# A transformer layer with conditioned norms: c first on its queue, the last tile in two column steps, one load for two chunks, and a new order of all engines

## The chip, the cores and the metric

The kernel runs on one core of a Trainium2 chip. The metric is the device time of one execution in microseconds (us). Where this text names engines: PE multiplies matrices (PEld is its loading of weights, which overlaps it), ACT is ScalarE, DVE is VectorE, POOL is GpSimd, SP is SyncE, which here only issues DMAs.

## What is computed

One layer over 2048 tokens of 448 features, in bf16: a local, dilated attention (16 heads of 28, 8 keys at a distance of 2 each) and a feed-forward of 1792, each behind a layernorm whose shift, scale and gate come from a small vector c.

```python
x = A_x                                             # (1, 2048, 448)
mod = (_silu(c) @ w_mod).reshape(c.shape[0], 6, 1, -1)
sa, ca, ga, sb, cb, gb = (mod[:, i] for i in range(6))
h = _layernorm(x) * (1 + ca) + sa
x = x + ga * _A_ref(h, A_wqkv, A_wo)                # q, k, v = h @ wqkv; softmax over keys s, s-2, ..., s-14; @ wo
h = _layernorm(x) * (1 + cb) + sb
x = x + gb * (_silu(h @ B_w1) @ B_w2)
```

## The kernel before

**Tiles.** The tokens are cut into 4 chunks of 512, each of 4 tiles of 128 rows (two neighbouring tokens share a partition, so even and odd tokens, which never attend to each other, are separate tiles). Everything stays in SBUF: x (`x_all`, 16 tiles), all weights, the queries and keys of all tokens (`qk`).

**Stages.** For each chunk `norm1` (L640) makes statistics on DVE (L497) or ACT (L501, L507), the root on POOL (L513), a normed copy `xn` (L523 to L527), its transpose on PE (chunk 0, L564) or by DMA (chunks 1 to 3, L588), and scale and shift (L571, L573, L593, L595). `project` (L659) multiplies h with the query and key weights (L668) and the value weights (L688). The query and key weights are first copied from `wqk` into `wp`, where each head of 28 columns is padded to 32 (`pad`, L601 to L606); the last 64 rows of both have a load of their own, `wqk3` (L381). Attention goes by 9 blocks of 112 queries and the two parities: `logits` (PE L716, exponentials on ACT L724, a mask on DVE L748), `values` (PE L774, a normalisation on DVE L779 and L780, a DMA transpose L784), `out_proj` (PE L804, DVE L807). The feed-forward goes by chunks: `ffn1` (PE L831, Silu on ACT L839), `ffn2` (PE L854, an add on DVE L859, a store L862). `last_tile` (L875) replaces `ffn2` for the last 128 rows: its output columns are in two accumulators of 224, one added to x on DVE (L892), the other with x already in it (a matmul with the identity, L882) copied on ACT (L895); one store follows (L898). The gates of the modulation are multiplied into `wo` (L916) and `w2` (L920); `mrow` (L477) is the row of modulations from which they come.

**Halves of rows.** 448 is three and a half times 128. The projections, `out_proj` and `ffn1` therefore use matmuls on 64 rows in pairs that run side by side: `phases` (L609) makes a "straight" part of 8 matmuls and a "crossed" part of 6, which waits (L630) until the straight part has left PE.

**Order.** Every step is an operation of `Plan` (L106) with a number. A search made offline wrote the order of all operations into `ORDER` (L44): the numbers in turn, with the engine where there is a choice (`v` is DVE, `a` is ACT) and the PSUM banks after slashes. `emit` (L205) issues them so. Each engine, and SP's queue of DMAs, runs its own operations in that order and waits by semaphore for what they need. The durations and the `lag` in the calls of `P.op` are for the search; where the order is written out they are not used. A second path (`safe`), which runs only if a softmax sum leaves its range, plans its order anew.

**First loads.** ACT's queue issues the second pair of tiles of x, then c (L368, L369), and loads the table for Silu (L370). SP's queue issues the first pair, the first half of `w_mod`, then weights and chunks of x, all by `load` (L361, L362). A DMA to chunk k of x is one of `ld_x` (L383).

Of the kernel before, what the change touches and what calls it, by code (L numbers as in the profile page):

```python
# [10 lines left out]
ALU = mybir.AluOpType  # L11
ACTF = mybir.ActivationFunctionType
# [21 lines left out]
NC = 4  # L34
# [203 lines left out]
def layer(ctx, tc, io, safe):  # L238
# [24 lines left out]
    def onet():  # L263
        return psum[:, P.bank("one"), :]
# [103 lines left out]
    act_q = [P.op(("none", 0.0), lambda o: nc.scalar.dma_start(**first_x(1)))]  # L368
    act_q.append(P.op(("none", 0.0), lambda o: nc.scalar.dma_start(out=c4[:], in_=c.rearrange("o (k p) -> (o k) p", p=KM)), act_q[-1:]))  # L369
    ld_c = [P.op(("none", 5200.0), lambda o: S.preload_act_table(ACTF.Silu), act_q[-1:])]  # L370
    ld_x = [[load(224, **first_x(0)), P.op(("none", 4400.0), none, act_q[:1])]]
# [11 lines left out]
    ld_x += [[load(448, x_all[:, 4 * k:4 * k + 4, :].rearrange("p (i t) d -> p i (t d)", t=2), x_view[k], late)] * 2 for k in range(1, NC)]  # L383
# [225 lines left out]
    def phases(mm, n, deps, split=False):  # L609
# [25 lines left out]
        return box, a, P.op(("pe", 3 * step), crossed, [a], mode=1, lag=300.0)  # L635
# [239 lines left out]
    def last_tile(k, j, u):  # L875

        box, n = {}, D // 2

        def part(o, f0, f1):
            if f0 == 0:  # L880
                box["ps"] = [onet(), onet()]
                T.matmul(box["ps"][1][:, 0:n], lhsT=ident[:], rhs=x_all[:, u, n:D], start=True, stop=False)  # L882
            for f in range(f0, f1):
                for i in range(2):
                    T.matmul(box["ps"][i][:, 0:n], lhsT=hid[:, k % 2, f % 2, f // 2, 128 * j:128 * j + 128], rhs=w2[:, f // 2 + 7 * (f % 2), n * i:n * i + n],  # L885
                             start=(f + i == 0), stop=(f == NF - 1))
# [4 lines left out]
        def add(o):  # L891
            V.tensor_tensor(out=box["o"][:, 0:n], in0=box["ps"][0][:, 0:n], in1=x_all[:, u, 0:n], op=ALU.add)  # L892

        def move(o):
            S.copy(out=box["o"][:, n:D], in_=box["ps"][1][:, 0:n])  # L895

        def store(o):
            nc.sync.dma_start(out=out_view[u // 4, u // 2 % 2, u % 2], in_=box["o"][:])  # L898
        prev = None
        for f0, f1 in ((0, 4), (4, 8), (8, 12), (12, 14)):  # L900
            need = silus[k][f0 // 2:f1 // 2] + w2_gated + ([x1_done[u]] if f0 == 0 else [])
            prev = P.op(("pe", 194.0 * (f1 - f0) + (98.0 if f0 == 0 else 0.0)), lambda o, f0=f0, f1=f1: part(o, f0, f1), need + [prev], take=("one", "one") if f0 == 0 else ())
            if f0 == 0:
                first = prev
# [119 lines left out]
```

## Time and profile before

| | us |
|---|---|
| median of three runs | 171.99 (170.29 to 173.71) |
| the profiled execution | 170.89 |
| its span, from first to last instruction | 169.2 |
| busy: PE, ACT, DVE, POOL | 160.8, 116.4, 99.1, 15.5 |

The profile is of one execution, so sums are made against its 170.89, of which 169.2 is the span. Times in its rows count from the start of the span. PE's matmuls are pipelined and their ends are modelled, so that PE can be marked busy while it is behind its pace; its pace is read from groups that run without a wait. In a row of a timeline stand start, length, engine, line, operation, tile written and tiles read, shape, count, and in brackets how long the engine was idle before it and what ended that.

The costliest groups of instructions are PE's in the feed-forward:

```profile
L831 PE MATMUL psum<-h,w 64*128 64x512 bf16 x392 | 43.7, 376 | 0.0
L854 PE MATMUL psum<-w,both 128*128 128x448 bf16 x210 | 42.1, 353 | 0.0
L839 ACT ACTIVATE both<-psum 128x1024 bf16<-128x1024 f32 x28 | 27.3, 1021 | 13.6 <-PE psum L831 13.6
```

Behind the bar stand busy time and the mean of one in ns (pipelined matmuls overlap, so the mean is longer than the distance from one to the next), then the idle time of the engine ahead of the group.

### The profile page before, as it was taken

How to read it: one execution, taken by the hardware profiler on the slowest of the kernel's cores; microseconds unless marked ns; L12 is line 12 of the kernel's file. 1: busy time of each engine (PE TensorE's matmuls, PEld its weight loads, DVE VectorE, ACT ScalarE, POOL GpSimd, SP SyncE). 2: the span in 40 equal slices, each digit the busy share in tenths (PEclk: the TensorE clock that was granted, in tenths of full speed). 3: DMA queues.
4: the chain of work that ended last, by engine and by line, in shares of the span. 5: the costliest groups of instructions: out<-in, count | busy, mean ns of one | idle time of the engine just before them, and what ended most of it. 6: DMA issues, size and time to landing. Idle time of an engine off the chain costs nothing.

```text
span 169.2 us, 4278 instructions
## 1 busy us (share of the span) xinstructions
PE 160.8 (95%) x1763; PEld 79.9 (47%) x1764; DVE 99.1 (59%) x259; ACT 116.4 (69%) x166; POOL 15.5 (9%) x38
## 2 busy tenths in 40 slices
PE   7878999999999999999999999999999999999990
PEld 2344444353465554554464454564444454444670
DVE  2788899999988859475476309972950405100120
ACT  3676999899779967879996989484429903248000
POOL 4313112010000410011000000021001100000000
PEclk9999999999999999999999999999999999999999
DMA  5994999859994453500614001226410061100022
GB/s 180 251 324 171 190 303 164 265 154 101 142 248 109 112 103 76 169 0 9 119 27 111 2 0 31 54 63 117 113 54 6 0 124 38 49 0 0 27 62 68
DMA packets 32312, 17.48 MB, mean 103 GB/s; under 512 B 24157, under 2 KB 31453, under 8 KB 32285
## 3 DMA queue, kind: packets, MB, share of 16 engines
q1 hardware_dynamic: 32132, 16.90, 42.9%
q8 instruction: 16, 0.26, 0.7%
q10 hardware_dynamic: 152, 0.23, 0.4%
q14 instruction: 12, 0.09, 0.2%
HBM read 9.12 MB, written 1.84 MB: 65 GB/s over the span
## 4 chain that ended last, share of the span: by engine, by line
PE 74%; DMA 9%; DVE 7%; ACT 5%; issue 2%; SPq 0%
PE psum L831 25%; PE psum L854 24%; PE psum L804 7%; PE psum L668 6%; DMA wqk<-in_A_wqkv_dram 5%; PE psum L688 4%; PE psum L774 4%; PE psum L716 2%; DMA x_all<-in_A_x_dram 2%; DMA oT<-o 2%; DVE p L748 2%; PE psum L885 2%; ACT both L501 1%; ACT wp L603 1%; DVE wqk L595 1%
## 5 line engine op out<-in xcount | busy, mean ns | idle before, releaser
L831 PE MATMUL psum<-h,w 64*128 64x512 bf16 x392 | 43.7, 376 | 0.0
L854 PE MATMUL psum<-w,both 128*128 128x448 bf16 x210 | 42.1, 353 | 0.0
L839 ACT ACTIVATE both<-psum 128x1024 bf16<-128x1024 f32 x28 | 27.3, 1021 | 13.6 <-PE psum L831 13.6
L724 ACT ACTIVATE p<-psum 128x896 bf16<-128x896 f32 (+1 forms) x36 | 31.7, 935 | 5.0 <-PE psum L716 4.7
L831 PEld LDWEIGHTS <-w 64*128 64x128 bf16 x392 | 19.3, 94 | 22.2 <-issue 0.7
L854 PEld LDWEIGHTS <-both 128*128 128x128 bf16 x210 | 19.6, 98 | 19.1 <-issue 1.6
L513 POOL TENSOR_TENSOR rs<-rs,negh 128x2 f32<-128x2 f32 x16 | 12.5, 778 | 118.0 <-DVE rs L510 82.6
L748 DVE TENSOR_TENSOR p<-p,maskb 128x1792 bf16<-128x1792 bf16 (+1 forms) x18 | 19.5, 1099 | 4.8 <-ACT p L724 4.8
L859 DVE TENSOR_TENSOR ot<-psum,x_all 128x448 bf16<-128x448 f32 x15 | 9.2, 618 | 20.2 <-PE psum L854 15.9
L668 PE MATMUL psum<-h,wp 64*128 64x512 bf16 x168 | 19.8, 377 | 0.5 <-ACT wp L603 0.4
L668 PEld LDWEIGHTS <-wp 64*128 64x128 bf16 x224 | 10.4, 94 | 12.8 <-ACT wp L603 0.9
L507 ACT ACTIVATE mrow<-x_all,mv 128x448 bf16<-128x448 bf16 x16 | 10.7, 668 | 3.4 <-DVE mv L504 3.0
L804 PE MATMUL psum<-wo,oT 64*128 64x448 bf16 x112 | 12.7, 350 | 0.1
L593 ACT ACTIVATE h<-h,modc 128x512 bf16<-128x512 bf16 x7 | 5.5, 806 | 10.2 <-DMA h<-xn 10.2
L672 ACT CAST qk<-psum 128x1024 bf16<-128x1024 f32 x12 | 12.0, 1018 | 0.6 <-PE psum L668 0.6
L688 PE MATMUL psum<-wv,h 64*128 64x448 bf16 x98 | 11.3, 350 | 1.2 <-DMA wv<-in_A_wqkv_dram 1.1
L807 DVE SCALAR_TENSOR_TENSOR x_all<-psum,x_all 128x448 bf16<-128x448 f32 x16 | 9.5, 619 | 3.6 <-PE psum L804 3.6
L780 DVE TENSOR_TENSOR o<-psum,rc 112x448 bf16<-112x448 f32 (+1 forms) x18 | 11.2, 624 | 0.6
L779 DVE RECIPROCAL rc<-psum 112x16 f32<-112x16 f32 (+1 forms) x18 | 4.5, 251 | 10.2 <-PE psum L774 9.5
L774 PEld LDWEIGHTS <-p 128*128 128x128 bf16 x288 | 8.2, 96 | 3.3 <-issue 1.7
L774 PE MATMUL psum<-v,p 128*128 128x29 bf16 x288 | 9.0, 176 | 0.0
L595 DVE TENSOR_SCALAR h<-h,modc 128x512 bf16<-128x512 bf16 x17 | 6.1, 406 | 4.8 <-DMA h<-xn 4.6
(95 smaller groups left out, 144.6 us busy)
## 6 DMA issues: line engine op xcount, KB each, us to landing
out_dram<-ot SPq DMA_DIRECT2D x16, 112.0 KB, 1.8
both<-in_w_mod_dram SPq DMA_DIRECT2D x1, 1568.0 KB, 8.4
x_all<-in_A_x_dram SPq DMA_DIRECT2D x3, 448.0 KB, 8.1
w<-in_B_w_dram SPq DMA_DIRECT2D x3, 448.0 KB
w<-in_B_w_dram SPq DMA_DIRECT2D x1, 896.0 KB, 7.0
both<-in_w_mod_dram SPq DMA_DIRECT2D x2, 392.0 KB, 5.7
w<-in_B_w_dram SPq DMA_DIRECT2D x1, 672.0 KB, 5.4
wv<-in_A_wqkv_dram SPq DMA_DIRECT2D x2, 224.0 KB, 8.5
```

The costliest lines, as they stand in the source:

```text
L513: G.tensor_tensor(out=rs[:, j:j + n], in0=rs[:, j:j + n], in1=negh[:, 0:n], op=ALU.pow)
L668: return T.matmul(ps[:, j, :], lhsT=w.rearrange("p h d -> p (h d)"), rhs=h[rows, :, t, 128:128 + CP], start=start, stop=stop)
L672: copy_on(o)(out=qk[:, :, g, :, s0:s0 + CP], in_=ps.rearrange("p j (t s) -> p j t s", t=2))
L688: T.matmul(ps[:, par, 0:D], lhsT=h[rows, par, t, b0:b0 + 128], rhs=wv[rows, t, :], start=start, stop=stop)
L724: S.activation(out=out_, in_=ps[:, :, 0:4 * nq].rearrange("p j (g q) -> p j g q", q=nq), func=ACTF.Exp, scale=SCALE)
L748: V.tensor_tensor(out=p, in0=p, in1=maskb[:, 1 if b == 0 else 0, 0:nq].unsqueeze(1).to_broadcast([128, H, nq]), op=ALU.mult)
L774: T.matmul(ps[:, h, 0:DH + 1], lhsT=p[:, at:at + 128], rhs=v[:, h, 0:DH + 1], start=True, stop=True)
L780: V.tensor_tensor(out=box["o"][0:nq, off:off + D].rearrange("p (h d) -> p h d", d=DH), in0=ps[0:nq, :, 0:DH], in1=r.unsqueeze(2).to_broadc ...
L804: T.matmul(ps[par][:, 0:D], lhsT=oT[rows, t, par, s0:s0 + 128], rhs=wo[rows, par, t, :], start=start, stop=stop)
L831: return T.matmul(ps[:, j, :], lhsT=w, rhs=h[rows, :, t, :], start=start, stop=stop)
L839: silus[k].append(P.op(("act", 904.0), lambda o, i=i, box=box: S.activation(out=hid[:, k % 2, :, i, :], in_=box["ps"], func=ACTF.Silu), [m ...
L854: T.matmul(box["ps"][:, 0:D], lhsT=hid[:, k % 2, f % 2, f // 2, 128 * j:128 * j + 128], rhs=w2[:, f // 2 + 7 * (f % 2), :], start=(f == 0) ...
```

## The change

1. On ACT's queue c is issued before the tiles of x. In the new order the Silu of c is ACT's first instruction.
2. Chunks 2 and 3 of x come in one DMA of 896 KB, where each had its own of 448.
3. `last_tile` has three accumulators, of 224, 112 and 112 columns. PE runs the first over all 14 steps, then the other two. The first is added on DVE and stored while PE works on the rest; of the rest one part is added on DVE and the other (with x in it by the identity matmul) copied on ACT, and a second store follows.
4. `ORDER` is another one throughout. On SP's queue `wqk3` comes behind the other `wqk` loads (before: ahead of `wv`). ACT, DVE, POOL and PE have other orders, and some operations with a choice are on the other engine: the cast of `mrow` is on DVE, the pad of `wqk3` on ACT.
5. `lag` and some durations for the search are other numbers.

```diff
 ORDER = (
-    "1 60/0 46 47 6 0 4 7 5 80 81 8 2 9 61 63 66 88 3 69 89 70/2 62 10 22 16 48 90 67 18 19 82 55 20 87 91 71 73/2 83 84 21 11 85v 74 97/3/4 86v 98 64 92 "
...
+    "1 0 4 58/0 5 78 7 2 8 44 45 79 46 59 6 9 10 22 3 67 68/2 23 69 61 20 86 18 19 71/2 87 88 49 50 80 21 64 60 65 85 89 11 72 12 81 63 82 83v 95/3/4 84v "
...
-    act_q = [P.op(("none", 0.0), lambda o: nc.scalar.dma_start(**first_x(1)))]
-    act_q.append(P.op(("none", 0.0), lambda o: nc.scalar.dma_start(out=c4[:], in_=c.rearrange("o (k p) -> (o k) p", p=KM)), act_q[-1:]))
+    act_q = [P.op(("none", 0.0), lambda o: nc.scalar.dma_start(out=c4[:], in_=c.rearrange("o (k p) -> (o k) p", p=KM)))]
+    act_q.append(P.op(("none", 0.0), lambda o: nc.scalar.dma_start(**first_x(1)), act_q[-1:]))
...
-    ld_x += [[load(448, x_all[:, 4 * k:4 * k + 4, :].rearrange("p (i t) d -> p i (t d)", t=2), x_view[k], late)] * 2 for k in range(1, NC)]
+    ld_x.append([load(448, x_all[:, 4:8, :].rearrange("p (i t) d -> p i (t d)", t=2), x_view[1], late)] * 2)
+    ld_x += [[load(896, x_all[:, 8:16, :].rearrange("p (k i t) d -> p k i (t d)", i=2, t=2), x_view[2:4].rearrange("c p i n -> p c i n"), late)] * 2] * 2
...
-        return box, a, P.op(("pe", 3 * step), crossed, [a], mode=1, lag=300.0)
+        return box, a, P.op(("pe", 3 * step), crossed, [a], mode=1, lag=230.0)
...
     def last_tile(k, j, u):
-        box, n = {}, D // 2
+        box, cut = {}, (0, D // 2, 3 * D // 4, D)
...
+            for f in range(f0, f1):
+                for i in range(i0, i1):
+                    T.matmul(box["ps"][i][:, 0:cut[i + 1] - cut[i]], lhsT=hid[:, k % 2, f % 2, f // 2, 128 * j:128 * j + 128], rhs=w2[:, f // 2 + 7 * (f % 2), cut[i]:cut[i + 1]],
+                             start=(f == 0 and i < 2), stop=(f == NF - 1))
...
+        for i0, i1 in ((0, 1), (1, 3)):
+            for f0, f1 in ((0, 8), (8, 14)):
...
+            if i0 == 0:
+                ot = P.op(("none", 0.0), hold, [first], take=("out",))
+                done = [P.op(("dve", 310.0), lambda o: add(o, 0), [prev, ot], give=((first, "one"),))]
+                sp(550.0, lambda o: store(o, 0, 1), done, dma=(390.0, 500.0, 250.0))
+            else:
+                ad = [P.op(("dve", 195.0), lambda o: add(o, 1), [prev, ot], give=((first, "one"),)), P.op(("act", 150.0), move, [prev, ot], give=((first, "one"),))]
+                sp(550.0, lambda o: store(o, 1, 3), ad, 1200.0, ((ot, "out"),), (390.0, 500.0, 250.0))
```

More of the change, by code (lines that the diff above doesn't have):

```diff
@@ L367, in first_x @@
         return dict(out=x_all[:, 2 * i:2 * i + 2, :].rearrange("p t d -> p (t d)"), in_=x_view[0, :, i, :])
[L368 to L371, printed above, removed]
+    act_q = [P.op(("none", 0.0), lambda o: nc.scalar.dma_start(out=c4[:], in_=c.rearrange("o (k p) -> (o k) p", p=KM)))]
+    act_q.append(P.op(("none", 0.0), lambda o: nc.scalar.dma_start(**first_x(1)), act_q[-1:]))
+    ld_c = [P.op(("none", 3900.0), lambda o: S.preload_act_table(ACTF.Silu), act_q[-1:])]
+    ld_x = [[load(224, **first_x(0)), P.op(("none", 4800.0), none, act_q[-1:])]]
     def load_mod(k0, k1, c0, c1, after=()):
@@ L875, in last_tile, with part @@
     def last_tile(k, j, u):
-        box, n = {}, D // 2
-        def part(o, f0, f1):
+        box, cut = {}, (0, D // 2, 3 * D // 4, D)
+        def part(o, f0, f1, i0, i1):
             if f0 == 0:
-                box["ps"] = [onet(), onet()]
-                T.matmul(box["ps"][1][:, 0:n], lhsT=ident[:], rhs=x_all[:, u, n:D], start=True, stop=False)
+                box.setdefault("ps", []).extend(onet() for _ in range(i0, i1))
+                if i1 == 3:
+                    T.matmul(box["ps"][2][:, 0:cut[3] - cut[2]], lhsT=ident[:], rhs=x_all[:, u, cut[2]:cut[3]], start=True, stop=False)
@@ L883, in part @@
             for f in range(f0, f1):
-                for i in range(2):
-                    T.matmul(box["ps"][i][:, 0:n], lhsT=hid[:, k % 2, f % 2, f // 2, 128 * j:128 * j + 128], rhs=w2[:, f // 2 + 7 * (f % 2), n * i:n * i + n],
-                             start=(f + i == 0), stop=(f == NF - 1))
+                for i in range(i0, i1):
+                    T.matmul(box["ps"][i][:, 0:cut[i + 1] - cut[i]], lhsT=hid[:, k % 2, f % 2, f // 2, 128 * j:128 * j + 128], rhs=w2[:, f // 2 + 7 * (f % 2), cut[i]:cut[i + 1]],
+                             start=(f == 0 and i < 2), stop=(f == NF - 1))
@@ L888, in hold, with add @@
         def hold(o):
             box["o"] = outb[o["slot"]["out"]]
-        def add(o):
-            V.tensor_tensor(out=box["o"][:, 0:n], in0=box["ps"][0][:, 0:n], in1=x_all[:, u, 0:n], op=ALU.add)
+        def add(o, i):
+            V.tensor_tensor(out=box["o"][:, cut[i]:cut[i + 1]], in0=box["ps"][i][:, 0:cut[i + 1] - cut[i]], in1=x_all[:, u, cut[i]:cut[i + 1]], op=ALU.add)
         def move(o):
-            S.copy(out=box["o"][:, n:D], in_=box["ps"][1][:, 0:n])
-        def store(o):
-            nc.sync.dma_start(out=out_view[u // 4, u // 2 % 2, u % 2], in_=box["o"][:])
@@ L899, in last_tile @@
[L899 to L904, printed above, removed]
-        ot = P.op(("none", 0.0), hold, [first], take=("out",))
-        ad = P.op(("dve", 310.0), add, [prev, ot], give=((first, "one"),))
@@ L907, in last_tile, with store @@
-        mv = P.op(("act", 242.0), move, [prev, ot], give=((first, "one"),))
-        sp(550.0, store, [ad, mv], 1200.0, ((ot, "out"),), (390.0, 500.0, 360.0))
+            S.copy(out=box["o"][:, cut[2]:cut[3]], in_=box["ps"][2][:, 0:cut[3] - cut[2]])
+        def store(o, i, n):
+            nc.sync.dma_start(out=out_view[u // 4, u // 2 % 2, u % 2][:, cut[i]:cut[n]], in_=box["o"][:, cut[i]:cut[n]])
+        prev, done = None, []
+        for i0, i1 in ((0, 1), (1, 3)):
+            for f0, f1 in ((0, 8), (8, 14)):
+                need = silus[k][f0 // 2:f1 // 2] + w2_gated + ([x1_done[u]] if f0 == 0 else [])
+                prev = P.op(("pe", 97.0 * (f1 - f0) + (50.0 if i0 and not f0 else 0.0)), lambda o, a=(f0, f1, i0, i1): part(o, *a), need + [prev], take=("one",) * (i1 - i0) if f0 == 0 else ())
+                if f0 == 0:
+                    first = prev
+            if i0 == 0:
[5 more added lines that the diff above has]
+                sp(550.0, lambda o: store(o, 1, 3), ad, 1200.0, ((ot, "out"),), (390.0, 500.0, 250.0))
```

44 rows, old and new, of the table ORDER are left out of this document.

## The prediction

> **What bounds the kernel now.** I read the totals first, then the chain of work that ended last, then the stretches.
>
> ```profile
> span 169.2 us, 4278 instructions
> PE 160.8 (95%) x1763; PEld 79.9 (47%) x1764; DVE 99.1 (59%) x259; ACT 116.4 (69%) x166; POOL 15.5 (9%) x38
> PE 74%; DMA 9%; DVE 7%; ACT 5%; issue 2%; SPq 0%
> ...
> 39.34 3.02 DMA oT<-o
> 42.41 0.93 PE psum L804 x7
> ...
> 165.11 0.37 DVE ot L892
> ...
> 42.40:165.10 122.70, 122.69 (x1315) 62.73 (x1315) 62.72 (x157) 80.76 (x108) 6.76 (x8) 1.00 0.31 68
> ```
>
> The first two rows are the page's totals, the third its chain of waits by engine; then three pieces of that chain in order of time (start, length, what). The last row is one stretch of the table by windows: of the 122.70 us between 42.40 and 165.10, PE is busy for 122.69, at a granted clock of 1.00, while DVE and ACT are busy for 62.72 and 80.76. The chain of waits says the same: from 42.41 on every piece is PE's, up to the last add. In these 123 us an edit gains only by giving PE less to do, and loses whatever it makes PE wait. The remaining 46 us are the head (PE waits for loads, then works with small stalls) and a tail of 4 us. The head, in the timeline of each engine, with two pieces of the chain from later on as the measure of PE's pace:
>
> ```profile
> 12.16 3.27 PE L688 MATMUL psum<-wv,h 64*128 64x448 bf16 x28 [1.05 <-DMA wv<-in_A_wqkv_dram]
> 15.86 7.97 PE L668 MATMUL psum<-h,wp 64*128 64x512 bf16 x70 [0.43 <-ACT wp L603]
> 23.76 0.73 PE L716 MATMUL psum<-qk 28*128 28x128 bf16 x16
> 28.31 0.40 PE L716 MATMUL psum<-qk 28*128 28x128 bf16 x16
> 37.42 1.04 PE L668 MATMUL psum<-wqk,wp 64*128 64x512 bf16 x8 [0.22 <-ACT qk L672]
> 41.94 1.39 PE L804 MATMUL psum<-wo,oT 64*128 64x448 bf16 x8
> ...
> 14.03 1.78 ACT L603 COPY wp<-wqk 128x896 bf16<-128x896 bf16 x2 [1.29 <-DMA wqk<-in_A_wqkv_dram]
> ...
> 14.73 0.39 DVE L603 COPY wp<-wqk 128x896 bf16<-128x896 bf16 x1 [0.79 <-DMA wqk<-in_A_wqkv_dram]
> ...
> 65.32 0.57 PE psum L804 x6
> 143.59 10.68 PE psum L831 x98
> ```
>
> PE starts the value projections at 12.16, when `wv` has landed, and the query and key projections at 15.86, when ACT has made its second padded copy of `wqk` (14.03 + 1.78 = 15.81). These copies waited for `wqk`: one part was there at 14.03, the other at 14.73. So the DMA of the weights sets 15.86.
>
> From there to 42.41 PE is marked busy but is not at its pace. At 10.68/98 = 0.109 us a matmul 70 projections need 7.63, and took 7.97 (0.34 lost); the logits at 23.76 took 0.73 where the like group at 28.31 took 0.40 (0.33); 0.22 is idle at 37.42; the output projection took 1.39 for 8 matmuls, where 8 need 0.57 × 8/6 = 0.76 (0.6 lost). That is 1.5 us which another order could win in this stretch, and no more.
>
> **The change, part by part.**
>
> *c first on ScalarE's queue, one table load less.* Two things happen to ACT: the tile of x on its queue is issued after c, and the Silu table is loaded before anything else, so that the first of two loads goes.
>
> ```profile
> 0.81 0.41 ACTq L368 DMA_DIRECT2D x_all<-in_A_x_dram  x1
> 1.25 0.58 ACTq L369 DMA_DIRECT2D c<-in_c_dram  x1
> 1.86 1.28 ACT L501 ACT_TABLE_LOAD   x1 [1.86 <-issue]
> 5.14 1.28 ACT L370 ACT_TABLE_LOAD   x1
> 9.46 2.84 ACT L571 ACTIVATE h<-psum,modc 128x256 bf16<-128x256 bf16 x6 [2.03 <-PE psum L564]
> ```
>
> The tile of x is issued about 0.6 later (c's issue took 0.58), and the second table load no longer stands between c and its silu (1.28). Both matter only for h at 9.46 to 12.30, and h is needed together with `wv` (12.16) and the padded `wqk` (15.86), so the net gain of 1.28 − 0.58 = 0.7 is hidden by the weights; I take 0. Were that cover gone, it would be worth up to 0.7; if h came later instead, 15.86 − 12.30 = 3.5 of cover are there, less the 3.3 of value projections that want h first.
>
> ```profile
> 14.00:15.00 1.00, 1.00 (x14) 0.61 (x11) 0.27 (x1) 0.97 (x2) 0.65 (x1) 1.00 0.39 142
> 15.00:16.00 1.00, 0.57 (x7) 0.11 (x4) 1.00 (x5) 1.00 (x2) 0.00 (x0) 1.00 0.19 67
> 16.00:17.00 1.00, 1.00 (x12) 0.44 (x10) 1.00 (x3) 1.00 (x3) 0.00 (x0) 1.00 0.05 18
> ...
> 30.57 0.56 ACT L477 CAST mrow<-psum 128x448 bf16<-128x448 f32 x1
> 16.41 0.62 DVE L497 BATCH_NORM_STATS2 st<-x_all 128x6 f32<-128x448 bf16 x1
> 16.51 0.58 ACT L501 ACTIVATE both<-x_all 128x448 bf16<-128x448 bf16 x1
> ```
>
> *The order of SP's queue: the small `wqk3` load moves from ahead of `wv` to behind the other `wqk` loads.* All the weights that PE needs at 15.86 still come before x's later chunks, so the bytes ahead of the last of them are the same, and the last lands near 14.7 as before. But it is now the 448-column part. Its pad stands on ACT; the 896-column pads land earlier and two of three are on DVE, which needs 0.39 for one. A 448-column instruction on ACT takes 0.56 (L477), so the pads end at 14.7 + 0.6 = 15.3 instead of 15.81: **−0.5**. Bounds: −0.7 if no more than the wait to 14.73 and one copy of 0.39 are left (15.12), +0.8 if the last part lands only at 16.0. For the second speaks that in the last column but one of the three windows the DMA share falls to 0.39, 0.19 and 0.05 of the sixteen engines, while loads are still landing: the last ones end on few engines. Which load put those behind, no row tells.
>
> *Two chunks of x in one load.* The bytes are the same, but the first reader of chunk 2 waits for all 896 KB. Before, DVE and ACT turn to chunk 2 at 16.41 and 16.51, while the queue is busy until nearly 17. With the load whole at about 16.9 DVE waits 0.5, ACT 0.4. In the chain of waits ACT and then DVE lead from the weights to the DMA at 39.34, so this is no gain and may be a loss of 0.5; it goes into the ends of the next term.
>
> *The new order up to the first output projection.* ACT gives the cast of `mrow` (0.56) to DVE, DVE gives a norm to ACT; the first logits stand one straight part (8 × 0.109 = 0.9) further back, the first output projection a whole projection (14 matmuls, 1.5), which covers the wait for the transposes of o behind the 0.6 above. In their place: the gates now wait for DVE's cast of `mrow`, which stands behind a mask and a cast of v; SP issues the transpose of chunk 3's first half before `w2`'s first load, and `w13` after the first transposes of o, so that `w13` stands ahead of the transpose of chunk 3's second half. I take **0**, with −1.5 (all stalls gone) and +1.5 (as many again) as ends. On top, two straight parts in this stretch, not one, are followed at once by their own crossed part. The 0.34 above holds the one there was: **+0.2**, bounds 0 and +0.34.
>
> *PE's changes of kind.* PE runs three kinds of matmul: on 64 rows in pairs, on 28 rows (logits), on all 128. A change costs time:
>
> ```profile
> 45.18 0.50 PE psum L774 x16
> 55.71 0.67 PE psum L804 x6
> 85.21 0.39 PE psum L774 x16
> 110.86 0.79 PE psum L774 x32
> ```
>
> The same 16 matmuls take 0.50 behind a projection and 0.39 behind logits; the same six matmuls of L804 0.67 behind logits and 0.57 in a row of their kind (65.32, above). Counted in the two programs' PE order from the first value projection on, changes that cost this (all but those that leave logits) are 45 before and 40 after: 5 × 0.10 = **−0.5**. [...] Bounds: −0.3 (five at half of it) to −0.55 (at 0.11).
>
> *The last tile in two column steps.* Before, 28 matmuls of 224 columns in two accumulators, then add and copy side by side, then one store:
>
> ```profile
> 162.81 0.77 PE psum L885 x8
> 161.33 0.62 DVE L859 TENSOR_TENSOR ot<-psum,x_all 128x448 bf16<-128x448 f32 x1 [1.97 <-PE psum L854]
> 165.10 0.39 DVE L892 TENSOR_TENSOR ot<-psum,x_all 128x224 bf16<-128x224 f32 x1 [0.23 <-PE psum L885]
> 165.55 0.33 SPq L898 DMA_DIRECT2D out_dram<-ot  x1
> DMA to landing us min/median/max: 2.2/2.2/2.2
> ```
>
> After: 14 of 224 columns and 28 of 112. 128x29 ran at 0.79/32 = 0.025 each, below half of the 0.096 of 224 columns (0.77/8), so 112 columns can be had at 0.05 and the sum stays; at worst the 14 extra cost 14 × 0.05 = +0.7. I take 0, near the small ones. The first half's add (0.39) and store (0.33 to issue) lie beside the second step's 28 matmuls (1.4). The last add shrinks by half the slope between 448 and 224 columns, (0.62 − 0.39)/2 = 0.12. The last store carries half the bytes; 2.2 to landing stays or falls a little (0 to −0.3, I take −0.1). **−0.2**. [...]
>
> *No cost:* `lag` and the planner's durations are not read where the order is written out, and the second, safe path is not run.
>
> **Sum**, against the profiled execution (170.89, of which the span is 169.2): −0.5 + 0 + 0.2 − 0.5 − 0.2 = −1.0, so 169.9. That execution is 1.1 below the median of the three runs shown (171.99); on their scale 171.0.
>
> **Rivals.** Two rows more for their prices:
>
> ```profile
> 18.57 0.58 ACT L501 ACTIVATE both<-x_all 128x448 bf16<-128x448 bf16 x1
> w<-in_B_w_dram SPq DMA_DIRECT2D x1, 672.0 KB, 5.4
> ```
>
> 1. *The stalls go as well.* The 1.5 us of the stretch from 15.86 to 42.41 are won: 171.99 − 2.5 = 169.5. For it: the output projection stands further back. Against it: DVE is dense there and gets a cast more. 0.13.
> 2. *Chunk 2 becomes the bound: slower than before.* If the 896 KB land not by 17 but when ACT came to chunk 3 before (18.57, which waited for nothing), DVE stands still from the end of its work on chunk 1 and starts chunk 2 2.1 later than at 16.41. All of it goes on, because the chain runs over ACT and DVE up to the DMA at 39.34: −1.0 + 2.1 = +1.1, 173.1. It decides from a landing at 16.41 + 1.0 = 17.4 on. For it: a load whose last part trails on few engines ends late whole. Against: the same bytes had landed before 18.57. 0.25.
> 3. *A hole in the dense part.* The new order puts the gating of the last w2 rows on DVE right ahead of the second feed-forward's first use (they are among the last things DVE does ahead of it). If `w2`'s second load is issued only when it is needed, its whole 5.4 to landing is exposed: 171.0 + 5.4 = 176.4. It decides from the point where the load is later than the first part of the feed-forward ends. Against: PE did not wait once there, with DVE idle half the time. 0.08.
> 4. *Only the removed work shows* (the forecast, with its ends): 0.54.
>
> **How the numbers follow.** The likeliest is 171.0; its own range is 170.3 to 172: the stretch at a third of its ends (±0.5), the pads between −0.7 and 0. 8 in 10: down to 169.4 (rival 1), up to 173.2 (rival 2). About 2%, 3.4 us, is what a measurement of this kernel can tell from no change: its three runs differ by as much. Faster by more than that needs 168.5: all of rival 1 and more, 0.05. Slower by more needs 175.4: rival 3 and some of rival 2's tail, 0.08. Within: 0.87.
>
> **What would show it.** First projection of queries at about 15.3, the pad of `wqk3` ending just before. PE busy without a gap from about 42 on, and the sum of it 0.5 shorter. First statistics of chunk 2 on DVE at about 16.9. The last add at about 0.27. It is wrong if PE waits for more than 0.5 in sum after 42.4, if the first projection comes after 16, or if chunk 2's statistics come after 17.4.

## The result, and the profile after

The changed kernel is slower: 176.38 us median of 6 runs (174.72 to 176.78) against 171.25 (170.29 to 173.71), a ratio of 1.029 (95% interval 1.023 to 1.036). Forecast was 171.0. The profiled execution took 174.72, its span is 172.9 where it was 169.2. So the profile shows 3.7 us of the loss, and the median run lost 1.7 more than the profiled one; a second profile, further down, shows where.

The page's totals of the changed kernel and its chain of waits by engine, and then two pieces of that chain in order of time (start, length, what):

```profile
span 172.9 us, 4310 instructions
PE 161.0 (93%) x1778; PEld 80.1 (46%) x1778; DVE 97.4 (56%) x255; ACT 119.0 (69%) x170; POOL 15.9 (9%) x38
PE 69%; DMA 16%; DVE 8%; ACT 1%; issue 1%; POOL 1%; SPq 0%; ACTq 0%; DVEq 0%
```

```profile
25.07 5.96 DMA wqk<-xn
43.77 7.33 DMA h<-xn
```

PE's busy time is the same to 0.3 us, but the DMA's share of the chain rose from 9% to 16%, and these two pieces of it are transposes. The timeline of the changed kernel shows what stood around the second, with the rows for the head and the last add that the prediction named:

```profile
14.23 0.38 PE L669 MATMUL psum<-h,wp 64*128 64x512 bf16 x2
14.46 0.56 ACT L606 COPY wp<-wqk 128x448 bf16<-128x448 bf16 x1 [0.59 <-DMA wqk<-in_A_wqkv_dram]
15.08 0.39 PE L669 MATMUL psum<-h,wp 64*128 64x512 bf16 x2 [0.47 <-ACT wp L606]
16.76 0.63 DVE L498 BATCH_NORM_STATS2 st<-x_all 128x6 f32<-128x448 bf16 x1 [0.77 <-DMA x_all<-in_A_x_dram]
...
41.05 0.60 SPq L362 DMA_DIRECT2D w<-in_B_w_dram  x1
42.46 1.21 SPq L785 DMA_TRANSPOSE oT<-o  x1
43.77 2.42 SPq L589 DMA_TRANSPOSE h<-xn  x1
47.46 2.82 PE L689 MATMUL psum<-wv,wqk 64*128 64x448 bf16 x28
51.12 2.22 ACT L594 ACTIVATE h<-h,modc 128x512 bf16<-128x512 bf16 x3 [3.78 <-DMA h<-xn]
52.42 0.39 PE L669 MATMUL psum<-h,wp 64*128 64x512 bf16 x2 [2.14 <-DVE o L781]
53.40 0.82 PE L669 MATMUL psum<-h,wp 64*128 64x512 bf16 x6 [0.59 <-ACT h L594]
...
168.47 0.27 DVE L894 TENSOR_TENSOR ot<-psum,x_all 128x112 bf16<-128x112 f32 x1 [0.44 <-PE psum L887]
```

The load at 41.05 is `w13`. Behind it comes a transpose of o, then the transpose of chunk 3's second half, issued at 43.77 and landed at 51.10. PE ends its last work that doesn't need it at 50.28 and then waits 2.14 and 0.59: ACT had waited 3.78 for the same transpose, DVE 2.55 (its reciprocal and norm of o, which the first wait names, stand behind a modulation that needs it too).

The windows of the changed kernel, and of the kernel before at the same place (columns: PE, PEld, DVE, ACT, POOL busy, granted clock, DMA share, GB/s; the last row of each runs from the first value projection to the last matmul):

```profile
42.00:50.00 8.00, 8.00 (x134) 4.40 (x130) 6.40 (x14) 5.35 (x7) 0.00 (x0) 1.00 1.08 63
50.00:54.00 4.00, 1.27 (x12) 0.33 (x8) 2.84 (x7) 2.88 (x4) 0.00 (x0) 1.00 0.83 222
10.97:168.41 157.44, 152.77 (x1711) 76.39 (x1710) 90.84 (x225) 114.15 (x160) 11.66 (x18) 1.00 0.43 91
```

```profile
42.00:50.00 8.00, 7.89 (x146) 4.13 (x148) 6.94 (x18) 5.88 (x8) 0.00 (x0) 1.00 1.09 201
12.16:165.10 152.94, 151.89 (x1696) 75.85 (x1695) 91.01 (x226) 109.08 (x152) 11.37 (x17) 1.00 0.41 93
```

From 42 to 50 the DMA share is above 1 in both, but 63 GB/s were moved after and 201 before: after, packets were under way that hardly moved. The last rows give the sum. PE's first value projection is 1.19 earlier; its idle time from there to the last matmul is 157.44 − 152.77 = 4.67 where it was 1.05 (+3.62); its busy time there is 152.77 against 151.89 (+0.88); from the last matmul to the end it is 4.5 against 4.1 (+0.4). Together +3.7. Of the idle time 2.73 are the hole above, and 0.77 stand near 32 us, where the gates wait for the cast of `mrow`.

### The profile page after: what moved, and what is told of

Same layout as the page of the kernel before. It is cut to its first block, busy times and chain, and to the rows that moved or that the text cites. A ratio compares the mean times of both kernels' runs of the same rounds, so it can differ in the third digit from the quotient of the medians.

```text
span 172.9 us, 4310 instructions
## 1 busy us (share of the span) xinstructions
PE 161.0 (93%) x1778; PEld 80.1 (46%) x1778; DVE 97.4 (56%) x255; ACT 119.0 (69%) x170; POOL 15.9 (9%) x38
## 4 chain that ended last, share of the span: by engine, by line
PE 69%; DMA 16%; DVE 8%; ACT 1%; issue 1%; POOL 1%; SPq 0%; ACTq 0%; DVEq 0%
PE psum L832 25%; PE psum L855 24%; DMA x_all<-in_A_x_dram 8%; PE psum L669 6%; PE psum L805 5%; DMA h<-xn 4%; DMA wqk<-xn 3%; PE psum L775 3%; PE psum L689 2%; PE psum L717 2%; PE psum L887 2%; ACT h L594 1%; DVE st L498 1%; DVE o L781 1%; DVE qk L673 1%
## 5 line engine op out<-in xcount | busy, mean ns | idle before, releaser
L832 PE MATMUL psum<-h,w 64*128 64x512 bf16 x392 | 44.2, 376 | 0.0
L855 PE MATMUL psum<-w,both 128*128 128x448 bf16 x210 | 42.4, 353 | 0.0
L669 PE MATMUL psum<-h,wp 64*128 64x512 bf16 x168 | 20.8, 377 | 3.3 <-DVE o L781 2.1
L514 POOL TENSOR_TENSOR rs<-rs,negh 128x2 f32<-128x2 f32 x16 | 12.8, 804 | 119.9 <-DVE rs L511 79.8
L594 ACT ACTIVATE h<-h,modc 128x512 bf16<-128x512 bf16 x11 | 8.4, 806 | 10.0 <-DMA h<-xn 10.0
L596 DVE TENSOR_SCALAR h<-h,modc 128x512 bf16<-128x512 bf16 x13 | 4.7, 407 | 7.1 <-DMA h<-xn 7.1
```

Source lines behind the costliest of these rows:

```text
L514: G.tensor_tensor(out=rs[:, j:j + n], in0=rs[:, j:j + n], in1=negh[:, 0:n], op=ALU.pow)
L669: return T.matmul(ps[:, j, :], lhsT=w.rearrange("p h d -> p (h d)"), rhs=h[rows, :, t, 128:128 + CP], start=start, stop=stop)
L832: return T.matmul(ps[:, j, :], lhsT=w, rhs=h[rows, :, t, :], start=start, stop=stop)
L855: T.matmul(box["ps"][:, 0:D], lhsT=hid[:, k % 2, f % 2, f // 2, 128 * j:128 * j + 128], rhs=w2[:, f // 2 + 7 * (f % 2), :], start=(f == 0) ...
```

## The experiments

The theory, read from the traces and put to the test below: `w13` (224 KB) and `wqk3` (112 KB) are narrow loads. Their access pattern in DRAM has an outermost dimension of 2 (two bands of 64 rows), and they run on few of the 16 engines; a transpose uses more of them and waits, on those few, for what was issued ahead of it. It rests on two kinds of records, neither of which names an engine. Those of completion: in the changed kernel `w13` reports once at 42.1 and then twice at 48.2, where the 448 KB load of w1 issued at 46.24 reports 16 times (52.2 to 52.3) and the transpose of chunk 3's second half 16 times as well (50.9 to 51.1). And those of packets: the 128 rows of `w13`, of 1792 bytes each, go two at a time for 4.7 of their 5.4 us (from 45.5 to 47, when no others begin, they fill 12.8% of the 16 engines' time, two engines' worth), and 24 of the transposes' 64 packets of 256 bytes that begin between 45 and 46 take 2.8 to 3.0 us, where most take 0.02. Rival A: chunk 3 is late because the 896 KB load makes x late. Rival B: the 448 KB load of w1 issued beside the transpose holds it up. All ratios are to the kernel before, run beside each.

**w13 early.** One load moved on SP's queue, to where it stood before:

```diff
-"... 169v 244 40 276 277 ... 292/2/3 324 38 208v 302 ..."
+"... 169v 244 40 38 276 277 ... 292/2/3 324 208v 302 ..."
```

> The changed kernel with one load moved on SP's queue: w13 (224 KB) is issued right behind w2's first load, as in the kernel before, not ahead of the transposes of o and of chunk 3's second half. All other orders are the changed kernel's. Theory (w13 is a narrow load, spread over few of the 16 DMA engines, and what is queued behind it on those engines waits): the transpose of chunk 3's second half lands 3 to 4.5 us after its issue instead of 7.3, PE's idle time at L669 between 50 and 54 us falls from 2.7 us to under 0.8, and the span falls from 172.9 to 169.6 to 170.8; ratio to before 1.00 to 1.01. Part of it may come back as a stall at the out-projection near 41, where the kernel before had 0.5 us of them. Rival A (the 896 KB load makes x late, and chunk 3's chain with it): nothing changes, the transpose still lands near 51, ratio 1.025 to 1.035. Rival B (the 448 KB w1 load and the transposes of o beside it hold the transpose up): still over 6 us to landing, ratio above 1.02.

Measured: 172.78 us, ratio 1.0085 (1.0051 to 1.0118), span 171.0. The same transpose among the DMA issues (the last number is the time to landing), and the windows:

```profile
h<-xn SPq DMA_TRANSPOSE x1, 4.3
```

```profile
42.00:50.00 8.00, 8.00 (x145) 4.45 (x135) 7.76 (x18) 7.30 (x10) 0.00 (x0) 1.00 0.76 137
50.00:54.00 4.00, 4.00 (x76) 2.14 (x74) 3.40 (x7) 4.00 (x6) 0.00 (x0) 1.00 0.48 101
```

The transpose lands in 4.3 instead of 7.3 and PE has no hole. The ratio falls by 0.021, 3.6 us: more than the hole's 2.7. The span was 0.2 above the expected 170.8, with 0.9 of waiting left at the gates. Rival B falls: the w1 load is issued right behind the transpose here as there.

**w13 behind.** The load two places later, behind chunk 3's transpose (token 38 from behind 324 to behind 246).

> The changed kernel with w13's load moved two places back on SP's queue, from ahead of the fifth transpose of o to right behind the transpose of chunk 3's second half. Theory (narrow load): that transpose lands 3 to 4 us after its issue at 42 to 43.5, that is by 47; the hole of 2.7 us in PE at 50 to 54 is gone or is moved to the next transposes of o, which are now the ones behind the load: one of those takes over 5 us to land. Span 169.8 to 171.5, ratio 1.00 to 1.015. Rivals A (late x) and B (the w1 load beside it): the transpose still lands after 49.5 and the hole stays, ratio 1.025 to 1.035.

Measured: 177.27 us, ratio 1.036 (1.030 to 1.043), span 174.1. PE's waits from 36 to 60 us (total, times, longest), and the windows behind the hole:

```profile
PE psum L805 <- DMA oT<-o: 2.0, 1, 2.0
```

```profile
58.00:60.00 2.00, 2.00 (x24) 0.82 (x14) 0.77 (x3) 1.82 (x4) 0.00 (x0) 0.58 0.76 208
60.00:62.00 2.00, 2.00 (x14) 0.69 (x10) 1.38 (x7) 1.81 (x4) 1.12 (x1) 0.57 0.00 0
```

The hole moved along with the load, as the theory said: now the out-projection waits 2.0 for the transposes of o behind it. The price was missed by a wide margin, 1.036 where at most 1.015 was expected. The windows show a part of it: after the hole PE ran for 4 us at a granted clock of 0.58, which is 4 × 0.42 = 1.7 us.

**w13 in two.** The same bytes at the same place, as two loads of 64 partitions:

```diff
-ld_1.append(load(224, w13[:], dram(B_w1, 128, F // 2, ((128, -F // 2, 2), (1, 0, K3), (0, 1, F // 2))), late, rate=0.3))
+ld_1.append(sp(800.0, lambda o: [nc.sync.dma_start(out=w13[half(h), :], in_=B_w1[128 + 128 * h:192 + 128 * h,
+    F // 2 - h * (F // 2):F - h * (F // 2)]) for h in range(2)], ...)[0])
```

> The changed kernel with w13's load written as two loads of 64 partitions each, one behind the other, at the same place on SP's queue; the same bytes. Theory, if it is the form of the load (two halves of 64 rows in one access pattern) that puts it on few DMA engines: the two halves are spread wider, 42 to 50 us moves clearly more than the 63 GB/s of the changed kernel, the transpose behind it lands within 4.5 us, span 169.8 to 171.2, ratio 1.00 to 1.012. If a load of 64 rows is as narrow as one of 2 times 64, or if the place alone matters: the transpose still takes over 6 us, ratio above 1.02. Rivals A and B: as for the place, no change.

Measured: 173.44 us, ratio 1.013 (1.008 to 1.018), span 171.2; the ratio is just past the 1.012 expected.

The DMA issues, and a window:

```profile
h<-xn SPq DMA_TRANSPOSE x1, 3.6
```

```profile
42.00:50.00 8.00, 8.00 (x144) 4.46 (x141) 7.75 (x18) 7.95 (x10) 0.00 (x0) 1.00 0.68 148
```

With the place untouched, the transpose lands in 3.6 (7.3 in the changed kernel) and 148 GB/s are moved (63 there). Each of the two loads now reports 16 times, by 44.1 and 44.9, and up to 16 of their packets go at once, where the one load reported three times and its packets went mostly two at a time. Bytes and place are the same, so it is the form of the load that holds up the transpose; how the form sets the number of engines was not shown.

**The other way round: w13 late in the kernel before.** Token 40, which is `w13` there, moved behind 36, right ahead of chunk 3's transposes.

> The kernel before with one load moved: w13 is issued right ahead of the transpose of chunk 3's second half (behind the first two transposes of o and a w1 load) instead of ahead of all of them; x is loaded in two 448 KB loads as ever there. Theory (narrow load): the transposes of chunk 3 land 6 to 8 us after issue instead of 4.7 to 5.2, a hole of 1 to 3 us opens in PE between 46 and 54 us, span 170 to 172.5, ratio 1.005 to 1.02. Rival A (late x): there is no late x here, so no hole, ratio 0.995 to 1.003, or faster by up to 0.5 us, since the out-projection near 41 no longer waits for w13.

Measured: 174.43 us, ratio 1.016 (1.008 to 1.024), span 172.8. PE's waits, and the windows behind the hole:

```profile
PE psum L688 <- DVE h L595: 2.0, 2, 1.8
```

```profile
54.00:56.00 2.00, 2.00 (x28) 0.86 (x25) 1.14 (x2) 0.73 (x2) 0.00 (x0) 0.50 0.42 79
56.00:58.00 2.00, 2.00 (x30) 1.07 (x28) 1.77 (x6) 0.43 (x1) 0.00 (x0) 0.70 0.55 149
```

The hole comes up in the kernel before as well, 2.0 us of it, with x loaded as ever. One transpose of chunk 3 took 8.1 (4.7 and 5.2 in the kernel before). Again the clock is down behind the hole, at 0.50 and 0.70 in the two windows.

**x in two loads.** w13 early, and the 896 KB load taken apart again.

```diff
-ld_x.append([load(448, x_all[:, 4:8, :]...)] * 2)
-ld_x += [[load(896, x_all[:, 8:16, :]...)] * 2] * 2
+ld_x += [[load(448, x_all[:, 4 * k:4 * k + 4, :]...)] * 2 for k in range(1, NC)]
```

> The changed kernel with w13's load early and x's chunks 2 and 3 in two loads of 448 KB again, one behind the other at the place of the 896 KB load. Theory: chunk 2's statistics start on VectorE 0.5 to 1 us earlier than the 16.8 us of the changed kernel, but nothing behind waits for them; span 170.7 to 171.3, ratio 1.006 to 1.010, as with w13 early alone. Rival A (the 896 KB load makes chunk 2 late and PE's waits between 25 and 42 us come from it): these waits shrink by 0.5 us or more, span under 170.5, ratio under 1.005.

Measured: 172.89 us, ratio 1.009 (1.005 to 1.013), as with w13 early alone. The first statistics of chunk 2 in the timeline:

```profile
16.47 0.62 DVE L497 BATCH_NORM_STATS2 st<-x_all 128x6 f32<-128x448 bf16 x1
```

Chunk 2's statistics start at 16.47 and not at 17.00 as with w13 early, and nothing is won in the ratio. (The profile is of this kernel's longest execution, 174.69, so its wait of 1.6 at the gates is no measure of the edit.) Rival A falls.

**wo behind the transposes, one store.** w13 early, and two more parts undone: the two loads of wo stand behind chunk 2's transposes again, and the last tile leaves in one store.

```diff
-"... 26 27 30 114a 28 29 173/2 111a 199 ... 174 231 ... 201 172a ..."
+"... 26 27 114a 173/2 111a 199 ... 174 231 ... 201 30 28 29 172a ..."
-sp(550.0, lambda o: store(o, 0, 1), done, ...)
+sp(550.0, none, done, ...)
-sp(550.0, lambda o: store(o, 1, 3), ad, ...)
+sp(550.0, lambda o: store(o, 0, 3), ad, ...)
```

> The changed kernel with w13's load early (as in the run before of that name, span 171.0, ratio 1.0085) and two more parts undone: the two loads of wo stand behind the transposes of chunk 2, as in the kernel before, and the last tile's rows leave in one store after both adds, its matmuls staying in two column steps. Theory (transposes wait behind the loads issued ahead of them; stores of 448-byte pieces are slow): chunk 2's transposes land 3.8 to 4.6 us after issue instead of 5.7, the 0.9 us that PE waits at the gates near 32 us shrink to under 0.5; from PE's last matmul to the end 4.0 to 4.2 us instead of 4.6; span 169.8 to 170.4, ratio 1.001 to 1.006. Rival (chunk 2 is late because x is): the transposes of chunk 2 still take over 5.3 us or the wait at the gates stays, and only the tail's 0.4 is won, ratio 1.006.

Measured: 171.63 us, ratio 1.000 (0.997 to 1.003), span 170.0. The transposes of chunk 2 among the DMA issues, and all of PE's waits from 15 us on:

```profile
wqk<-xn SPq DMA_TRANSPOSE x2, 4.8
```

```profile
PE psum L805 <- DMA oT<-o: 0.5, 2, 0.3
PE psum L669 <- ACT wp L606: 0.2, 1, 0.2
PE psum L669 <- ACT qk L673: 0.2, 1, 0.2
```

The transposes take 4.8 (5.7 with w13 early), not quite the 4.6 expected, and the wait at the gates (0.9 with w13 early) is gone. The chain was: two loads of wo, then the transposes, then DVE's modulation, then `mrow` behind it on DVE, then the gates on PE. The two edits together are worth 0.009, 1.5 us. The store was not what the expectation said: from the last matmul to the end it is still 4.5.

**Both narrow loads in two, in the changed kernel.** `wqk3` is split as `w13` is above.

> The changed kernel with both narrow loads, wqk3 (112 KB) and w13 (224 KB), each written as two loads of 64 partitions at its own place; every order is the changed kernel's. Theory (the form of the access pattern puts a load on few queues): as with w13 alone the hole at 50 to 54 us is gone; with wqk3 in two, what is queued behind it in the head (v's weights, x) lands earlier too, the first query projection starts at 15.0 to 15.4 and the waits between 25 and 42 us shrink a little; span 170.2 to 171.2, ratio 1.00 to 1.011. If wqk3 never held anything up: span as with w13 alone, 171.2, ratio 1.010 to 1.015.

Measured: 173.98 us, ratio 1.014 (1.006 to 1.022), span 172.0. The hole at 50 is gone, but nothing was gained over w13 alone (1.013), which is the second case of the expectation. In the profile the transposes of chunk 2 took 6.3 behind wo's loads, the gates waited 1.6, and the clock fell to 0.50 from 34 to 36 us.

**Both narrow loads in two, in the kernel before**, nothing else changed.

> The kernel before with wqk3 and w13 each written as two loads of 64 partitions at their places, nothing else. Theory: w13, issued there at 30, no longer holds wo's copy and the first transposes of o, so the 0.5 us that PE waited inside the out-projection at 42 are gone, and the transposes of chunk 3 land in 3.5 to 4.5 us instead of 4.7 to 5.2; span 168.3 to 169.0, ratio 0.993 to 0.999. If the narrow loads cost the kernel before nothing: ratio 0.998 to 1.002.

Measured: 169.64 us, ratio 0.988 (0.982 to 0.994), span 168.8: 1.2% faster than the kernel before, past the good end of what was expected. Its PE in the head:

```profile
10.63 3.18 PE L691 MATMUL psum<-wv,h 64*128 64x448 bf16 x28
14.19 2.98 PE L671 MATMUL psum<-h,wp 64*128 64x512 bf16 x26 [0.38 <-ACT wp L606]
```

The value projections start at 10.63 (12.16 in the kernel before) and the first query projection at 14.19 (15.86). Before, two pieces of `wqk3` reported only at 11.4 and 11.5, and `wv` and the rest of `wqk` stood behind them.

**wqk3 alone in two**, in the kernel before.

> The kernel before with wqk3 alone written as two loads of 64 partitions; w13 stays as it was. It tells which of the two loads gave the 1.2% of the run that had both. If wqk3 holds up v's and wqk's loads behind it: value projections start at 10.6 instead of 12.2, the first query projection at 14.2 instead of 15.9, and the first out-projection still waits for w13, later loss 0.5 us; ratio 0.987 to 0.993. If the gain came from w13: ratio 0.996 to 1.001, first query projection near 15.5.

Measured: 170.85 us, ratio 0.996 (0.992 to 0.999), span 169.0. PE in the head, and its waits from 15 to 60 us:

```profile
10.82 3.17 PE L691 MATMUL psum<-wv,h 64*128 64x448 bf16 x28
14.27 2.98 PE L671 MATMUL psum<-h,wp 64*128 64x512 bf16 x26 [0.27 <-ACT wp L606]
```

```profile
PE psum L807 <- DMA oT<-o: 1.0, 2, 0.8
```

The head is won as with both, but the earlier out-projection now waits 1.0 for the transposes of o, which stand behind the narrow `w13`. So `wqk3` wins the time and `w13` decides whether it is kept. The ratio of 0.996 is above the 0.993 expected and would also fit the expectation's other case, that the gain came from `w13`; the first query projection, at 14.27 where that case had 15.5, decides for `wqk3`.

**c first, in the kernel before** with both narrow loads in two; its orders are those of before.

> The kernel before with both narrow loads in two loads of 64 partitions, and c fetched first on ScalarE's queue, x's second pair behind it; its orders are those of before. The run without the c part had ratio 0.988 and span 168.8. If c first is worth nothing, as forecast: ratio 0.985 to 0.992. If the conditioning chain sets the head once the narrow loads are out of the way: up to 0.7 us faster, ratio 0.981 to 0.985. If x's second pair, later by one issue, sets it: up to 0.5 us slower, ratio 0.990 to 0.995.

Measured: 172.19 us, ratio 1.003 (1.000 to 1.006), where without c it was 0.988. The third guess has the direction, x's second pair, but 0.5 us was far too little for it. ACT's timeline (the statistics of x's second pair, then silu), the longest of PE's waits, and a window:

```profile
6.23 0.58 ACT L504 ACTIVATE both<-x_all 128x448 bf16<-128x448 bf16 x1 [3.16 <-DMA x_all<-in_A_x_dram]
8.21 0.29 ACT L427 ACTIVATE sc<-c 4x112 bf16<-4x112 bf16 x1
```

```profile
PE psum L432 <- ACT sc L427: 2.7, 1, 2.7
```

```profile
9.00:11.00 2.00, 2.00 (x28) 1.13 (x27) 1.10 (x6) 0.20 (x3) 1.56 (x8) 0.50 1.09 345
```

The pair of x, issued 0.58 later (1.39 against 0.81), lands 2.0 later: ACT starts on it at 6.23 and not at 4.22. By then SP has issued `w_mod` (from 1.27 on). In the kernels before and after, whose issues of these loads come at the same times (0.81 and 1.40 for the pair), the packets of this pair go from 1.99 to 3.66 and from 3.17 to 5.33, both times with packets of SP's loads beside them; that those hold up the later pair more is the author's guess, and no run tests it. In the order of before, silu stands behind these statistics on ACT, so PE waits 2.7 for c, which had come long before; and the clock falls there too. In the changed kernel the order has silu first (at 3.09), and x's pair, at 6.24, delays only itself.

**The changed kernel again**, as it is.

> The changed kernel as it is, a second time. Theory (a hole in PE of over 1.5 us is followed by some 4 us at about half the granted clock, in most executions): the hole of 2 to 3 us at 50 to 54 us is there, the spans are 172.5 to 175.5, and a profile that has a span over 173.5 shows granted clocks of 0.5 to 0.8 in the windows of 2 us right behind the hole, between 53 and 62 us, costing 1 to 2 us. Rival (the lower clock of its other runs is the chip's, or the tail's): no low clock behind the hole, or low clocks spread over the dense part. Ratio 1.02 to 1.035.

Measured: 176.93 us, ratio 1.030 (1.026 to 1.035), span of the profile 174.8. Its windows around the hole:

```profile
50.00:52.00 2.00, 0.54 (x6) 0.09 (x2) 0.34 (x2) 0.34 (x1) 0.00 (x0) 1.00 0.87 266
52.00:54.00 2.00, 0.46 (x4) 0.18 (x6) 1.97 (x6) 2.00 (x4) 0.00 (x0) 1.00 0.61 144
54.00:56.00 2.00, 2.00 (x24) 0.69 (x25) 1.45 (x2) 1.53 (x3) 0.00 (x0) 0.50 0.53 111
56.00:58.00 2.00, 2.00 (x38) 0.97 (x34) 0.12 (x1) 1.56 (x2) 0.00 (x0) 0.65 0.98 383
58.00:60.00 2.00, 2.00 (x38) 0.94 (x35) 1.93 (x6) 1.40 (x3) 0.00 (x0) 1.00 0.09 31
```

PE waits 2.4 and 0.6, and then runs at 0.50 and 0.65 for 4 us: 2 × 0.50 + 2 × 0.35 = 1.7 us. That is the difference between the first profile's run, in which the clock stayed at 1.00, and the median. So in such a run the hole costs twice.

**Mended.** The changed kernel with both narrow loads in two, wo's loads behind chunk 2's transposes, the cast of `mrow` ahead of chunk 2's modulation on DVE (token 122v from behind 31 to ahead of 207v), and one store.

> The changed kernel with four edits: both narrow loads in two loads of 64 partitions, the loads of wo behind chunk 2's transposes, the cast of mrow ahead of chunk 2's second modulation on VectorE, and one whole-row store for the last tile. c first, the 896 KB load of x and all other orders stay. Theory (the whole loss is loads ahead of transposes, and what PE waits for them): no hole over 0.5 us is left after 15 us, the clock stays at 1.0, span 169.2 to 170.2, ratio 0.992 to 1.001. If the new order has a cost of its own: PE still waits 1 us or more in sum after 15 us, span 170.3 or more, ratio above 1.003.

Measured: 171.68 us, ratio 1.000 (0.997 to 1.003), span 170.1. The only wait of PE between the first value projection and the last matmul, that window, the same window of the kernel before with both narrow loads in two, and the first DMA in the mended kernel's chain of waits:

```profile
PE psum L778 <- DVE p L752: 0.3, 1, 0.3
```

```profile
11.33:164.97 153.64, 152.76 (x1711) 76.70 (x1710) 90.71 (x225) 114.09 (x160) 11.64 (x18) 1.00 0.41 93
```

```profile
10.63:164.10 153.47, 151.98 (x1697) 76.08 (x1696) 91.95 (x230) 110.42 (x154) 11.64 (x17) 1.00 0.42 95
```

```profile
1.40 5.19 DMA x_all<-in_A_x_dram
```

No hole is left, and the time is that of the kernel before: the value projections start 0.83 earlier (11.33 against 12.16), but PE's busy time in its window is 152.76 against 151.89, and the tail is 5.1 against 4.1. The run with `w13` early, wo's loads behind the transposes and one store came to the same 1.000 with no load split. So the theory accounts for the loss against the kernel before.

It does not follow that the rest of the change costs nothing. The mended kernel has its narrow loads in two, and with them in two the kernel before has 0.988. Against that one the mended kernel is some 1.2% slower, 1.3 us in the spans (170.1 and 168.8): the value projections start 0.70 later, PE's busy time is 0.78 longer, the tail is 0.43 longer, and PE is idle 0.61 less. The chain of waits of the mended kernel begins with x's second pair, which c first makes late; the longer busy time and tail were not taken apart.

## Why the prediction was wrong

*What bounds the kernel.* Right: from 42 us on an edit loses whatever it makes PE wait. In the profile 2.73 of the 3.7 us came that way, and the prediction's own sign of being wrong (PE waits for more than 0.5 us after 42.4) is what showed it.

*The step that failed* is "The new order up to the first output projection": taken as 0, with +1.5 as its bad end. It named the move itself, "so that `w13` stands ahead of the transpose of chunk 3's second half", and gave it no price of its own. It bounded the new order only up to the first output projection, at 42, while the wait that this move made stands at 50 to 53, where the forecast counted no wait (only rival 3 has one there, for another load). It weighed stalls against stalls and counted queue time as bytes, where `w13` with 224 KB took 7.2 to land in the changed kernel and the 448 KB of w1 behind it 6.0. The move of wo's loads ahead of chunk 2's transposes it did not see. Measured, the waits it stands for are 2.73 (`w13` ahead of a transpose) and 0.77 (wo's loads ahead of chunk 2's transposes, and `mrow` behind their modulation on DVE), and to most executions the lower clock behind the hole adds 1.7 (the mean granted clock was 0.997 in the profiled run and 0.984 to 0.989 in the other five). The cover was to be priced as well: in the kernel before `w13` was issued 12 us ahead of those transposes, and that distance hid a load that takes 7 to 10 us (41.05 to 48.2 after, 30.25 to 40.4 before). The narrow loads were in sight: the pad's bounds rested on windows in which DMA shares trail off ("the last ones end on few engines. Which load put those behind, no row tells"). Runs with one load split at a time told it: `wqk3`, and further on `w13`.

*The pads and `wqk3`'s place*, −0.5: right in kind, and a little more than its good end of −0.7. ACT's pad ended at 15.0 (forecast 15.3), and the query projections went on at 15.08 behind it (15.86 before, forecast 15.3), after a first pair at 14.23. The value projections, which the forecast did not move, came at 10.97 instead of 12.16: in the kernel before `wv` stood behind the narrow `wqk3`, and the run with that load alone in two starts them at 10.82.

*c first*, 0: right for the changed kernel, where the weights were the cover that the prediction named (the query projections waited 0.47 for the pad), but by luck: the pair of x came 2.0 later, not 0.6. With the order of before and the narrow loads in two, c first costs 1.5% (1.003 against 0.988), and in the mended kernel, whose query projections no longer wait for the pad, the chain begins with this pair though its ACT has silu first.

*Two chunks of x in one load*: right. 16.76 where 16.9 was forecast, and no cost; rival 2, "Chunk 2 becomes the bound", falls with the run that undid it.

*Changes of kind and the extra pair*, −0.5 and +0.2: not seen. PE's busy time from the first value projection on was to fall by 0.3 and rose by 0.9 (as much in the mended kernel). Busy time here also holds time behind the pace (the 70 projections of the kernel before are marked busy for 7.97, where the prediction works out 7.63 at PE's pace), so this leaves the price of a change of kind open; no run changed only that.

*The last tile*, −0.2: the last add took 0.27 as forecast, the gain did not come. The changed kernel's last store was issued at once, but its issue took 1.42 where it had been 0.33, and 2.9 passed to landing in the median of the two stores where it had been 2.2 (the DMA issues of the changed kernel):

```profile
out_dram<-ot SPq DMA_DIRECT2D x2, 56.0 KB, 2.9
```

The run with one whole-row store took 1.23 to issue and 2.6 to land as well, so the shorter rows of the two stores are not shown to be the cause, and what makes this store slow is open.

*Rivals.* The third, "A hole in the dense part", had the shape, and by chance the time (176.4), but another place and cause: w2's second load held nothing up. The result lies above the range's 173.2 because a wait in the dense part had a chance of only 0.08.

## What to carry to other kernels

Before a load is moved on a queue, look at what now stands behind it and, in the trace, at how often the load reports and how long it takes to land. Here a load whose outermost dimension is 2 reported three times, and was better written as two with 64 rows each (a ratio of 1.013 against 1.029 for `w13` in the changed kernel, 0.988 against 1 for `w13` and `wqk3` in the kernel before) or kept far ahead of anything that waits (1.0085 for `w13` early in the changed kernel). What the order of one engine wins, the order of the queue that feeds it can lose, so price every load that passes a transpose, by its own time to landing. And price a hole in a dense TensorE stretch at more than its length, as the granted clock may fall behind it (here to 0.50 behind six of seven holes of 1.6 us or more, for 1.7 us more).

## What the runs showed that was not expected

- `w13`, 224 KB in a pattern that begins with a dimension of 2, took 7.2 us to land in the changed kernel and 10.1 in the kernel before. A transpose of chunk 3 behind it took 7.3 in the changed kernel and 8.1 in the kernel before with `w13` late, where it took 3.6 with `w13` in two and 4.7 to 5.2 in the kernel before. In the kernel before this was there all along: written as two each, the two narrow loads give a ratio of 0.988.
- Behind waits of PE of 1.6 to 2.7 us the granted clock fell to 0.50 and came back after 3.4 us (the trace's clock records; the windows above hold it in part), in six of the seven profiles that had such a wait: it did not in the changed kernel's first one, behind 2.1. Nor did it in those whose longest wait was 1.3 or less.
- 0.58 us later in issue made x's second pair land 2.0 us later, with the loads of `w_mod` issued in between.
